# An attention and gated-MLP kernel rewritten: one batched Gelu per segment, 20 score fills, pooled PSUM banks, one bank for two projections, DMA transposes

## The chip, the cores and the metric

The kernel runs on one core of a Trainium2 chip. The metric is device time in microseconds (us) of that core. A ratio always uses runs of the kernel before taken on the same chip in the same rounds. "Ratio" is the mean time of one kernel's fast runs over the mean time of the other's fast runs of the same rounds, so it is not quite the ratio of the medians that are quoted beside it. "us more" or "us less" than the changed kernel is a difference of medians from different jobs on different chips.

The engines are named as in the profile: PE (TensorE matmuls), PEld (its weight loads), DVE (VectorE), ACT (ScalarE), POOL (GpSimd), SP (SyncE, which here only issues DMAs). The program lists the instructions of each engine in one order, which is fixed when the kernel is built, by a list scheduler with estimated durations.

## The reference, cut to what matters

Both branches read the same x, 2048 tokens of 512 features. Four segments of 512 tokens are handled in order.

```python
def _A_ref(x, wq, wk, wv, wo, beta):              # 32 heads of 16
    for s in range(4):                            # segments of 512 tokens
        logits = einsum('bhqd,bhkd->bhqk', qs, ks) * scale + mask   # causal
        a_dot  = einsum('bhqk,bhkd->bhqd', softmax(logits), vs)
        a_mem  = phi(qs) @ M / (phi(qs) @ z + 1e-6)                 # memory of earlier segments
        outs.append(g * a_mem + (1 - g) * a_dot)
        M, z = M + phi(ks).T @ vs, z + phi(ks).sum()
    return concat(outs) @ wo
def _B_ref(x, w_gate, w_up, w_down):              # hidden size 1792 = 14 blocks of 128
    return (gelu(x @ w_gate) * (x @ w_up)) @ w_down                 # tanh form of gelu
gate = sigmoid((x * gate_w).sum(-1))
out  = gate * _A_ref(x, ...) + (1 - gate) * _B_ref(x, ...)
```

## The kernel before

Three parts of it matter for what follows.

The first is Gelu. For each of 14 blocks in each of 4 segments, the gate and up projections land in one fixed PSUM bank each, and six steps alternate between ACT and DVE:

```python
gc1  ACT  gs = copy(Gb)                         # out of PSUM
gu   DVE  ws = gs * gs
gz   DVE  ws = (ws + 1/C3) * gs
gt   ACT  ws = tanh(C_TANH*C3 * ws)
gh   DVE  ws = (ws + 1) * gs
gf   DVE  hT[ft] = 0.5 * ws * Ub                # frees the up-projection's bank
```

The second is the softmax. Scores of four heads go to four PSUM banks `X[0..3]` (one tensor, `psXALL`), one exp reads all four, POOL zeroes what is above the diagonal. There are three fills per unit and eight units per segment, so 96 exps:

```python
FILLS = [("A", [(0, 512, 0)], 512),
         ("B", [(1, 384, 0), (3, 128, 384)], 512),
         ("C", [(2, 256, 0)], 256)]              # this exp is only half as wide
```

The third is the use of the eight PSUM banks: four for scores, one each for gate (`Gb`), up (`Ub`), value products (`Pb`) and everything else (`Mb`). The down-projection and the O-projection both use `Mb`, one after the other, with an eviction each. phi of the keys (the positive form that the memory uses) and the attention outputs are transposed by PE through PSUM.

```python
task(f"bev{s}_{tile}", DVE, bsb = Mb * omgt)          # down-projection out of PSUM
...                                                   # O-projection into Mb again
task(f"fin{s}_{tile}", DVE, ostage = Mb * omgt + bsb)
```

The softmax here doesn't subtract the row's maximum and nothing guards it: scores larger than these inputs give would overflow.

Of the kernel before, what the change touches and what calls it, by code (L numbers as in the profile page):

```python
# [8 lines left out]


class InstrSpec:
    __slots__ = ("fn", "reads", "writes", "est", "dma_sem", "dma_inc", "waits", "task", "deps", "inc", "ins_name", "lat")

    def __init__(self, fn, reads=(), writes=(), est=0.1, dma_sem=None, dma_inc=16, lat=0.0):
        self.fn = fn
        self.lat = lat
        self.reads = tuple(reads)
        self.writes = tuple(writes)
        self.est = est
        self.dma_sem = dma_sem  # L20
        self.dma_inc = dma_inc
        self.waits = []
        self.task = None
        self.deps = []
        self.inc = False
        self.ins_name = None


class Task:
    __slots__ = ("name", "eng", "instrs", "est", "reads", "writes", "preds", "succs",  # L30
                 "prio", "start", "finish", "id", "order_bias", "lock_bank", "lock_gid", "lock_last", "lat")

    def __init__(self, name, eng, instrs, order_bias=0.0, lock=None):
        self.name = name
        self.eng = eng
        self.lock_bank, self.lock_gid, self.lock_last = lock if lock is not None else (None, None, None)
        self.instrs = list(instrs)
        for i in self.instrs:
            i.task = self
        self.est = sum(i.est for i in self.instrs) + 1e-3  # L40
        self.lat = max([i.lat for i in self.instrs] + [0.0])
        rs, ws = set(), set()
        for i in self.instrs:
            rs.update(i.reads)
            ws.update(i.writes)
        self.reads = rs
        self.writes = ws
        self.preds = set()
        self.succs = set()
        self.prio = 0.0  # L50
        self.start = None
        self.finish = None
        self.id = None
        self.order_bias = order_bias


class Sched:
    def __init__(self):
        self.tasks = []
        self._res_w = {}  # L60
        self._res_r = defaultdict(set)

    def add(self, task):
        task.id = len(self.tasks)
        deps = set()
        for r in task.reads:
            w = self._res_w.get(r)
            if w is not None and w is not task:
                deps.add(w)
        for w in task.writes:  # L70
            lw = self._res_w.get(w)
            if lw is not None and lw is not task:
                deps.add(lw)
            for rt in self._res_r.get(w, ()):
                if rt is not task:
                    deps.add(rt)
        for d in deps:
            task.preds.add(d)
            d.succs.add(task)
        for r in task.reads:  # L80
            self._res_r[r].add(task)
        for w in task.writes:
            self._res_w[w] = task
            self._res_r[w] = set()
        self.tasks.append(task)
        return task

    def schedule(self):
        tasks = self.tasks
        for t in reversed(tasks):  # L90
            best = 0.0
            for s in t.succs:
                if s.prio > best:
                    best = s.prio
            t.prio = t.est + best + t.order_bias
        n = len(tasks)
        npred = [len(t.preds) for t in tasks]
        ready_time = [0.0] * n
        ready = {e: [] for e in ENGINES}
        for t in tasks:  # L100
            if npred[t.id] == 0:
                ready[t.eng].append(t.id)
        cur = {e: 0.0 for e in ENGINES}
        done = 0
        order = []
        locked = {}
        while done < n:
            best = None
            best_e = None
            for e in ENGINES:  # L110
                lst = ready[e]
                if not lst:
                    continue
                ce = cur[e]
                bt = None
                bkey = None
                for tid in lst:
                    tt = tasks[tid]
                    blocked = False
                    for bk, gid in locked.items():  # L120
                        if bk in tt.writes and gid != tt.lock_gid:
                            blocked = True
                            break
                    if blocked:
                        continue
                    rt = ready_time[tid]
                    k = ((rt if rt > ce else ce), -tasks[tid].prio, tid)
                    if bkey is None or k < bkey:
                        bkey = k
                        bt = tid  # L130
                key = bkey
                if best is None or key < best:
                    best = key
                    best_e = e
            assert best is not None, "deadlock in task graph"
            st, _, tid = best
            ready[best_e].remove(tid)
            t = tasks[tid]
            if t.lock_bank is not None:
                if t.lock_last:  # L140
                    locked.pop(t.lock_bank, None)
                else:
                    locked[t.lock_bank] = t.lock_gid
            t.start = st
            t.finish = st + t.est
            cur[best_e] = t.finish
            order.append(t)
            done += 1
            for sc in t.succs:
                npred[sc.id] -= 1  # L150
                rt = t.finish + t.lat
                if ready_time[sc.id] < rt:
                    ready_time[sc.id] = rt
                if npred[sc.id] == 0:
                    ready[sc.eng].append(sc.id)
        self.order = order
        self.makespan = max(cur.values())
        self.eng_busy = {e: sum(t.est for t in tasks if t.eng == e) for e in ENGINES}
# [3 lines left out]
class Emitter:  # L162

    def __init__(self, nc, engmap):
        self.nc = nc
        self.engmap = engmap
        self.cnt = {}
        for e in (PE, ACT, DVE, POOL):
            self.cnt[e] = nc.alloc_semaphore(f"cnt_{e}")
# [5 lines left out]
    def plan(self, eng, spec):  # L175
        res = self.res
        deps = []
        for r in spec.reads:
# [3 lines left out]
        for w in spec.writes:  # L182
            st = res.get(w)
            if st is None:
                continue
            if st[0] is not None:
                deps.append(st[0])
            deps.extend(st[1].values())
        spec.deps = deps
        if spec.dma_sem is not None:  # L190
            sem = spec.dma_sem
            cur = self.dma_val.get(sem, 0) + spec.dma_inc
            self.dma_val[sem] = cur
            ref = ("d", sem, cur)
            rkey = ("d", id(sem))
        else:
            idx = len(self.streams[eng])
            ref = ("c", eng, idx)
            rkey = ("c", eng)
        for r in spec.reads:  # L200
            st = res.get(r)
            if st is None:
                st = [None, {}]
                res[r] = st
            st[1][rkey] = ref
        for w in spec.writes:
            res[w] = [ref, {}]
        self.streams[eng].append(spec)
        self.order.append((eng, spec))
        return ref  # L210

    def finalize(self):
        needed = {e: set() for e in (PE, ACT, DVE, POOL)}
        for eng, spec in self.order:
            for d in spec.deps:
                if d[0] == "c":
                    _, pe_, idx = d
                    if pe_ == PE and eng == PE:
                        continue
                    needed[pe_].add(idx)  # L220
        val = {}
        for e in (PE, ACT, DVE, POOL):
            c = 0
            vals = []
            for i, spec in enumerate(self.streams[e]):
                if i in needed[e]:
                    c += 1
                    spec.inc = True
                else:
                    spec.inc = False  # L230
# [3 lines left out]
        for eng, spec in self.order:  # L234
            req = {}
            for d in spec.deps:
                if d[0] == "c":
                    _, pe_, idx = d
                    if pe_ == PE and eng == PE:
                        continue  # L240
                    sem = self.cnt[pe_]
                    v = val[pe_][idx]
                else:
                    _, sem, v = d
                k = id(sem)
                if k not in req or req[k][1] < v:
                    req[k] = (sem, v)
            w = waited[eng]
            waits = []
            for k, (sem, v) in req.items():  # L250
                if w.get(k, -1) < v:
                    waits.append((sem, v))
                    w[k] = v
            spec.waits = waits

    def emit_stream(self, eng):
        e = self.engmap[eng]
        for spec in self.streams[eng]:
            for sem, val in spec.waits:
                e.wait_ge(sem, val)  # L260
            ins = spec.fn(e)
            try:
                spec.ins_name = ins.ins.name
            except Exception:
                spec.ins_name = None
            if spec.dma_sem is not None:
                ins.then_inc(spec.dma_sem, spec.dma_inc)
            elif spec.inc:
# [691 lines left out]
```

## Time and profile before

| | before |
|---|---|
| median time | 383.34 us (382.6 to 384.04, 3 runs) |
| profiled span | 381.4 us |
| exps, mean | 64 of 1.873 us, 32 of 1.021 us |
| DVE in the Gelu steps | 42.9 + 40.8 + 38.1 + 28.9 = 150.7 us |
| table loads on ACT | 1 of 1.283 us |

From the profile's page of the kernel before, part 1: the busy time of each engine and its share of the span.

```profile
span 381.4 us, 7327 instructions
PE 308.6 (81%) x2955; PEld 143.0 (38%) x3002; DVE 294.3 (77%) x635; ACT 253.6 (66%) x286; POOL 97.5 (26%) x147
```

From the same page, part 4, the chain of work that ended last, followed back from the end and summed by engine.

```profile
DVE 44%; PE 26%; ACT 20%; issue 6%; SPq 1%; POOL 1%; DMA 1%; POOLq 0%; ACTq 0%; DVEq 0%
```

No engine is full, and the chain goes from engine to engine with DVE in front. The groups view of the kernel before, by form, shows what they are busy with. Its columns are line, engine, operation, output<-input, shapes, count, then busy us and mean ns of one, then the engine's idle time just before these instructions and what ended it.

```profile
L769 ACT ACTIVATE pt<-psXALL 128x2048 bf16<-128x2048 f32 x64 | 119.9, 1873 | 19.1 <-PE psXALL L759 17.0 <-PE psP L788 1.0 <-POOL pt L776 0.4
...
L734 DVE SCALAR_TENSOR_TENSOR ws<-ws,gs 128x512 bf16<-128x512 bf16 x56 | 42.9, 765 | 1.5
L740 DVE SCALAR_TENSOR_TENSOR ws<-ws,gs 128x512 bf16<-128x512 bf16 x56 | 40.8, 729 | 2.9 <-ACT ws L737 2.0
...
L743 DVE SCALAR_TENSOR_TENSOR hT<-ws,psU 128x512 bf16<-128x512 bf16 x56 | 38.1, 681 | 7.8 <-PE psU L725 7.5
L737 ACT ACTIVATE ws<-ws 128x512 bf16<-128x512 bf16 x56 | 34.5, 627 | 27.2 <-DVE ws L734 27.1
...
L731 DVE TENSOR_TENSOR ws<-gs 128x512 bf16<-128x512 bf16 x56 | 28.9, 516 | 9.3 <-ACT gs L729 9.1
```

L734 and L731 are the cubic and the square, L740 the product, L743 the last product. Half of DVE's 294 us is Gelu. The Tanh (L737) stands idle 27 us for the cubic. The waits view (who waited for whom, us in total, times, longest) shows how that travels on to PE:

```profile
ACT ws L737 <- DVE ws L734: 27.1, 25, 4.2
ACT pt L769 <- PE psXALL L759: 26.6, 36, 2.2
PEld psU L725 <- DVE hT L743: 17.2, 23, 1.6
```

PE cannot start the next up-projection before DVE has emptied `Ub`. The second line is another loop. The timeline of the kernel before, 6 us of it (start, duration, engine, line), shows one turn:

```profile
173.68 1.86 ACT L769 ACTIVATE pt<-psXALL 128x2048 bf16<-128x2048 f32 x1
...
175.59 0.40 PE L759 MATMUL psXALL<-qT,kpad_1 32*128 32x384 bf16 x8 [0.18 <-ACT pt L769]
...
176.18 1.88 ACT L769 ACTIVATE pt<-psXALL 128x2048 bf16<-128x2048 f32 x1 [0.64 <-PE psXALL L759]
```

An exp ends, the scores of the next fill are computed into the same four banks (0.40 us), the next exp starts. The turn takes 2.50 us, of which ACT works 1.88.

### The profile page before, as it was taken

The page shows a single profiled execution, that of the slowest core. Times are in us where ns is not written, and L with a number is a line of the kernel's source. Part 1 is how long each engine was busy: PE and PEld are TensorE (multiplying, and loading weights), DVE is VectorE, ACT ScalarE, POOL GpSimd, SP SyncE. Part 2 cuts the span into 40 slices and gives each one's busy share as a digit, 9 for nine tenths or more (in the row PEclk, how much of TensorE's full clock was granted, in tenths as well). Part 3 has the DMA queues.
Part 4 walks back from the last instruction along what each step waited for, and adds up shares of the span by engine and source line. Part 5 has one row for each costly group of instructions (what it writes and reads, how often), then busy time and mean ns, then how long its engine had stood idle before and what let it go on. Part 6 is the DMA issues. An engine that isn't in the chain of part 4 may idle for free.

```text
span 381.4 us, 7327 instructions
## 1 busy us (share of the span) xinstructions
PE 308.6 (81%) x2955; PEld 143.0 (38%) x3002; DVE 294.3 (77%) x635; ACT 253.6 (66%) x286; POOL 97.5 (26%) x147
## 2 busy tenths in 40 slices
PE   4798887989878679788998878687998987688854
PEld 1344343444333244333443334343443324334431
DVE  0479898877866999997589899998587599985333
ACT  1579899875567367787567947787837765867630
POOL 7003433440022023233200312333300220433320
PEclk9999999999999987999999999999999999989968
DMA  3997000020010000001001000000000100000001
GB/s 86 353 363 110 2 3 2 1 57 2 0 43 15 0 2 2 0 16 44 2 0 41 15 0 3 2 2 0 3 2 14 43 1 2 2 0 2 2 0 55
DMA packets 17744, 12.26 MB, mean 32 GB/s; under 512 B 9776, under 2 KB 17712, under 8 KB 17712
## 3 DMA queue, kind: packets, MB, share of 16 engines
q1 hardware_dynamic: 17712, 11.81, 10.8%
q8 instruction: 23, 0.38, 0.4%
q14 instruction: 9, 0.07, 0.1%
HBM read 7.61 MB, written 2.10 MB: 25 GB/s over the span
## 4 chain that ended last, share of the span: by engine, by line
DVE 44%; PE 26%; ACT 20%; issue 6%; SPq 1%; POOL 1%; DMA 1%; POOLq 0%; ACTq 0%; DVEq 0%
ACT pt L769 11%; DVE ws L734 6%; DVE ws L740 6%; DVE hT L743 5%; PE psU L725 4%; PE psXALL L759 4%; DVE ws L731 4%; PE psM L838 4%; PE psM L861 3%; ACT kpad_1 L575 3%; PE psG L719 3%; ACT kpad_0 L575 2%; DVE ost L866 2%; PE psP L788 2%; DVE scr L816 2%
## 5 line engine op out<-in xcount | busy, mean ns | idle before, releaser
L769 ACT ACTIVATE pt<-psXALL 128x2048 bf16<-128x2048 f32 (+1 forms) x96 | 152.5, 1589 | 30.6 <-PE psXALL L759 26.6
L776 POOL TENSOR_SCALAR_AFFINE_SELECT pt<-pt 128x512 bf16<-128x512 bf16 x128 | 90.6, 709 | 267.8 <-ACT pt L769 226.9
L725 PE MATMUL psU<-xT,wu 128*128 128x512 bf16 x207 | 55.7, 388 | 15.5 <-DVE hT L743 11.1
L719 PE MATMUL psG<-xT,wg 128*128 128x512 bf16 x210 | 56.1, 386 | 8.6 <-ACT gs L729 7.0
L838 PE MATMUL psM<-wd,hT 128*128 128x512 bf16 x213 | 52.8, 379 | 3.1 <-DVE bsb L843 1.9
L737 ACT ACTIVATE ws<-ws 128x512 bf16<-128x512 bf16 x56 | 34.5, 627 | 27.2 <-DVE ws L734 27.1
L788 PE MATMUL psP<-vaug,pt 128*128 128x17 bf16 x1280 | 46.1, 171 | 6.9 <-POOL pt L776 3.5
L788 PEld LDWEIGHTS psP<-vaug,pt 128*128 128x128 bf16 x1280 | 40.3, 96 | 30.2 <-issue 16.9
L729 ACT ACTIVATE gs<-psG 128x512 bf16<-128x512 f32 x56 | 33.2, 593 | 17.2 <-DVE ws L740 8.9
L743 DVE SCALAR_TENSOR_TENSOR hT<-ws,psU 128x512 bf16<-128x512 bf16 x56 | 38.1, 681 | 7.8 <-PE psU L725 7.5
L734 DVE SCALAR_TENSOR_TENSOR ws<-ws,gs 128x512 bf16<-128x512 bf16 x56 | 42.9, 765 | 1.5
L740 DVE SCALAR_TENSOR_TENSOR ws<-ws,gs 128x512 bf16<-128x512 bf16 x56 | 40.8, 729 | 2.9 <-ACT ws L737 2.0
L731 DVE TENSOR_TENSOR ws<-gs 128x512 bf16<-128x512 bf16 x56 | 28.9, 516 | 9.3 <-ACT gs L729 9.1
L725 PEld LDWEIGHTS psU<-xT,wu 128*128 128x128 bf16 x224 | 18.2, 99 | 34.9 <-DVE hT L743 17.2
L719 PEld LDWEIGHTS psG<-xT,wg 128*128 128x128 bf16 x224 | 18.6, 98 | 28.8 <-ACT gs L729 10.6
L838 PEld LDWEIGHTS psM<-wd,hT 128*128 128x128 bf16 x224 | 19.2, 97 | 22.7 <-DVE bsb L843 2.2
L759 PE MATMUL psXALL<-qT,kpad_0 32*128 32x512 bf16 (+3 forms) x256 | 17.4, 302 | 8.7 <-ACT pt L769 8.2
L861 PE MATMUL psM<-wo,oT 128*128 128x512 bf16 x62 | 16.8, 393 | 7.8 <-DVE ost L866 5.2
L759 PE MATMUL psXALL<-qT,kpad_1 32*128 32x512 bf16 (+3 forms) x256 | 17.8, 311 | 4.5 <-ACT pt L769 4.3
L566 PE MATMUL psXALL<-xT,wk 128*128 128x512 bf16 x64 | 15.5, 394 | 5.4 <-DMA wk<-in_A_wk_dram 5.4
L803 DVE RECIPROCAL recip<-psP 128x16 f32<-128x16 f32 x32 | 8.1, 254 | 14.5 <-PE psP L788 14.3
L570 DVE CAST kT<-psXALL 128x512 bf16<-128x512 f32 x16 | 11.0, 688 | 10.7 <-PE psXALL L566 10.3
(81 smaller groups left out, 311.4 us busy)
## 6 DMA issues: line engine op xcount, KB each, us to landing
out_dram<-ost SPq DMA_DIRECT2D x16, 128.0 KB, 1.7
wg<-in_B_w_gate_dram SPq DMA_DIRECT2D x2, 896.0 KB, 9.4
wu<-in_B_w_up_dram SPq DMA_DIRECT2D x2, 896.0 KB, 10.6
wd<-in_B_w_down_dram SPq DMA_DIRECT2D x1, 1792.0 KB, 16.4
wk<-in_A_wk_dram SPq DMA_DIRECT2D x1, 512.0 KB, 4.7
wv<-in_A_wv_dram SPq DMA_DIRECT2D x1, 512.0 KB, 5.6
wq<-in_A_wq_dram SPq DMA_DIRECT2D x1, 512.0 KB, 6.4
wo<-in_A_wo_dram SPq DMA_DIRECT2D x1, 512.0 KB, 16.4
```

Source lines behind the costliest of these rows:

```text
L719: instrs.append(I(lambda e, kb=kb, ft=ft: e.matmul(Gb[:, :], wg[:, kb, ft * 128:(ft + 1) * 128], xT[sl][:, kb, :], start=(kb == 0), stop=( ...
L725: instrs.append(I(lambda e, kb=kb, ft=ft: e.matmul(Ub[:, :], wu[:, kb, ft * 128:(ft + 1) * 128], xT[sl][:, kb, :], start=(kb == 0), stop=( ...
L731: task(f"gu_{s}_{ft}", DVE, [I(lambda e, q=q: e.tensor_tensor(wsb[q][:, :], gsb[q][:, :], gsb[q][:, :], ALU.mult), reads=[("gsb", q)], wri ...
L734: task(f"gz_{s}_{ft}", DVE, [I(lambda e, q=q: e.scalar_tensor_tensor(out=wsb[q][:, :], in0=wsb[q][:, :], scalar=1.0 / C3, in1=gsb[q][:, :] ...
L737: task(f"gt_{s}_{ft}", ACT, [I(lambda e, q=q: e.activation(wsb[q][:, :], wsb[q][:, :], ACTF.Tanh, scale=C_TANH * C3), reads=[("wsb", q)], ...
L740: task(f"gh_{s}_{ft}", DVE, [I(lambda e, q=q: e.scalar_tensor_tensor(out=wsb[q][:, :], in0=wsb[q][:, :], scalar=1.0, in1=gsb[q][:, :], op0 ...
L743: task(f"gf_{s}_{ft}", DVE, [I(lambda e, q=q, ft=ft: e.scalar_tensor_tensor(out=hT[:, ft, :], in0=wsb[q][:, :], scalar=0.5, in1=Ub[:, :], ...
L759: instrs.append(I(lambda e, g=g, t=t, kb=kb, ncol=ncol, c0=c0, kp=kp: e.matmul(X[g][:, c0:c0 + ncol], kp[32 * g:32 * g + 32, t, kb * 128:( ...
L769: task(f"exp{s}_{u}_{fname}", ACT, [I(lambda e, slot=slot, ncols=ncols, xin=xin: e.activation(PT[slot][:, :, 0:ncols], xin, ACTF.Exp, scal ...
L776: minstrs.append(I(lambda e, mview=mview: e.affine_select(out=mview, in_=mview, compare_op=ALU.is_ge, fill=0.0, base=0, pattern=[[0, 4], [ ...
L788: instrs.append(I(lambda e, qb=qb, kb=kb, g=g, h=h, slot=slot, c0=c0: e.matmul(Pb[:, (qb * 4 + g) * 17:(qb * 4 + g) * 17 + 17], PT[slot][: ...
L838: instrs.append(I(lambda e, fb=fb, tile=tile: e.matmul(Mb[:, :], hT[:, fb, tile * 128:(tile + 1) * 128], wd[:, fb, :], start=(fb == 0), st ...
```

## The change

The intent is to take the Gelu arithmetic off DVE, to make fewer exps and all of them wide, to let all PE groups share the remaining banks, and to move transposes from PE to the DMA engines. The whole builder and its scheduler were rewritten, so the diff is 1500 lines. Its core, cut and condensed:

```diff
@@ Gelu: gate blocks are copied to hT, then one function in four chunks per segment @@
-  gc1, gu, gz, gt, gh, gf                       # six steps per block, see above
+  copy_out(f"Gev{s}_{ft}", ..., hT[sl][:, ft, :])             # by ACT or DVE, as the scheduler likes
+  CHUNKS = [(0, 2), (2, 6), (6, 10), (10, 14)]
+  e.activation(hT[sl][:, f0:f1, :], hT[sl][:, f0:f1, :], ACTF.Gelu_apprx_tanh)
+       # after = all exps of the segment; exps of the next segment come after the last chunk
+  task(f"Um{s}_{ft}", DVE, hT[ft] = up_bank * hT[ft])
@@ scores: 5 full fills per pair of units (20 per segment) in place of 6 @@
-  3 fills per unit, the third 256 columns wide
+  a0 = fill("A0", [(0, 0, 512, 0)], [0])
+  b0 = fill("B0", [(0, 1, 384, 0), (0, 3, 128, 384)], [0, 384])
+  cc = fill("C", [(0, 2, 256, 0), (1, 2, 256, 256)], [(0, 256)])   # both units
+  a1, b1 likewise
@@ PSUM: N_W = 3 pooled work banks; a group gets a bank when the scheduler starts it @@
-  Pb, Gb, Ub, Mb
+  Pb, banks = [psW0, psW1, psW2]
@@ O-projection and down-projection accumulate in one bank, one eviction @@
-  bev: bsb = Mb * omgt ; fin: ostage = Mb * omgt + bsb
+  ins  = [wo matmuls, start at kb == 0] + [wd matmuls, stop at fb == NFT - 1]
+  fin: ostage = bank * omgt                                    # ACT or DVE
@@ transposes of phi(k) and of the attention output (not the last segment's) @@
-  PE transpose into PSUM, DVE copy
+  e.dma_start_transpose(phkt[:, :, t*128:(t+1)*128], phk[:, t, :])
+  e.dma_start_transpose(oT[:, :, qt*128:(qt+1)*128], otok[sl][:, qt, :])
@@ start: weights of keys, queries, values on ACT's DMA queue, x on SP's @@
+  wdma("wk", ACT, ...); xdma(0); wdma("wq", ACT, ...); ...; wdma("wv", ACT, ...)
@@ phi is computed on two blocks at a time, padded keys are made from SBUF by DVE,
   denominators of the memory term in one small group, evictions may run on ACT or DVE,
   the scheduler adds hand-over times, a DMA model and bank allocation @@
```

## The prediction

> **What bounds it now.** No engine is full. The page gives a 381.4 us span: PE busy 308.6 (81%), DVE 294.3 (77%), ACT 253.6 (66%). The chain that ended last is 44% DVE, 26% PE, 20% ACT. The groups view shows why: each of the 56 Gelu blocks costs six steps that alternate between ACT and DVE: square 0.52, cubic 0.77, product 0.73, final product 0.68 us (2.7 us DVE), copy 0.59 and Tanh 0.63 us (1.2 us ACT). DVE Gelu work is 150.7 us. The waits view: Tanh waits 27 us for DVE, the up-projection's bank 17+11 us for the final DVE product. The timeline shows a second loop: the four score banks are single, so exp to exp is 1.88 + about 0.64 us (exp end, four score matmuls 0.4 us, exp).
>
> **Removed.** Square, cubic, product: 112.6 us DVE. Tanh: 34.5 us ACT. 16 down-projection evictions: 12.0 us DVE. Key padding from PSUM: 22 us ACT, replaced by a few us of DVE on wide SBUF operands. 24 phi and 12 output PE transposes with 12+12 DVE copies (about 10 us).
>
> **Added or moved.** One Gelu per 14 blocks, in four chunks: by the 0.83 us per 1000 elements that the 2048-wide exp's and 512-wide Tanh's times imply, about 6.8 us a segment, 27 us. Exp and this Gelu are, by the Trainium skill ("ScalarE: Activation LUTs", Table sets), likely in different table sets: 8 loads instead of 1. The trace's load took 1.283 us, as that page says; about 9 us more. Exp: 64x1873+32x1021 ns becomes 80x1873: 150 against 152.6 us: merging saves starts, not exp work.
>
> Estimated totals: ACT fixed work 200, DVE fixed work 125, movable evictions about 79 us: some 205 each. PE streaming hardly falls: 928 matmuls of 512 at 0.216 us (four in 0.87 us) is 200; value products 1280x0.027 = 35; scores about 20; rest 10: about 265 us. PE becomes the most loaded engine, the exp loop close behind.
>
> **Critical path, by stage.** Start: key weights are issued on ACT beside the transposes, so the first exp comes at about 13.5 us. Each segment has 20 exps at 2.52 us, plus about 0.25 us for scores queued behind other matmuls: 55 us; plus wide phi exps (6, 4, 2 of 1.05 us) and Gelu with two loads, 9.4 us. Segments: 70, 68, 66 us; PE needs about 66 in the middle ones, so it is nearly tied. Last exps 55. Then an exposed tail: Gelu, up-projection 12.3, down-projection 15.6, output 3: 34 us. Sum: 307 us. DVE's 150 us of relief thus gives about 75, because the exp loop and PE take over.
>
> **Prediction: 307 us, range 288 to 328.** Faster by over 2%: 0.96; within: 0.03; slower: 0.01.
>
> **Checks.** DVE busy 170 to 215 us, ACT 195 to 225, PE busy share 88% or more; 8 table loads; Gelu group near 27 us; exp x80 near 1.87 us with about 0.6 us idle before each; chain led by PE and ACT, DVE below 20%; no exp in the last 30 to 36 us.
>
> **What would make it wrong.** A fixed instruction order that fits reality badly: score matmuls held behind work matmuls whose bank is not free (three work banks), making exp gaps over 1 us. Transposing DMAs on one queue holding output or the memory products. Evictions assigned to ACT blocking exps. Gelu sharing exp's table, or PE filling the gaps better, would give 285 to 295.

## The result, and the profile after

The median is 317.69 us (315.19 to 318.75, 4 runs) against 383.09 us. The ratio is 0.8248, with a 95% interval from 0.8187 to 0.8309. Executions over 1.5% slower than the fastest of the same kernel are left out of the means. The prediction's range of 288 to 328 us holds it; the time is 10.7 us above the point of 307.

The kernel after, page parts 1 and 4, as shown of before:

```profile
span 315.7 us, 6866 instructions
PE 291.3 (92%) x2952; PEld 137.3 (43%) x2952; DVE 178.5 (57%) x360; ACT 219.7 (70%) x163; POOL 87.4 (28%) x130
...
PE 74%; DVE 10%; ACT 9%; DMA 3%; issue 2%; POOL 1%; SPq 0%; ACTq 0%; DVEq 0%
```

DVE lost 116 us and went from 44% to 10% of the chain. PE lost 17 us of busy time and now makes up three quarters of the chain. The groups view of the kernel after, by form:

```profile
L635 ACT ACTIVATE pt<-psXALL 128x2048 bf16<-128x2048 f32 x80 | 150.1, 1876 | 43.8 <-PE psXALL L628 39.3 <-POOL pt L646 4.2
...
L748 DVE TENSOR_TENSOR hT<-psW,hT 128x512 bf16<-128x512 f32 x56 | 37.0, 688 | 20.1 <-PE psW L372 20.0
L389 DVE CAST hT<-psW 128x512 bf16<-128x512 f32 x43 | 29.1, 689 | 11.8 <-PE psW L372 11.6
L733 ACT ACTIVATE hT<-hT 128x2048 bf16<-128x2048 bf16 x12 | 22.0, 1893 | 0.0
...
L733 ACT ACT_TABLE_LOAD x4 | 5.1, 1283 | 0.1
...
L635 ACT ACT_TABLE_LOAD x3 | 3.8, 1283 | 0.1
```

The Gelu chunks and the exps force seven more table loads of 1.283 us each. The last product (L748) now waits for PE; before, PE waited for it. The waits view after, for the two waits that answer to those of before (the Tanh's has no successor):

```profile
ACT pt L635 <- PE psXALL L628: 39.3, 44, 2.0
...
PEld psW L372 <- DVE hT L748: 3.6, 10, 0.8
```

The most useful view of this kernel is the table of windows, cut at the events that the program has in each segment: the first exp (17.13 us), and the Gelu stretch of each segment, from its table load to the next one's end. The columns are the stretch, its length, then busy us and instruction count of each engine, the granted TensorE clock, DMA share and GB/s.

```profile
0.00:17.13 17.13, 9.65 (x31) 3.12 (x32) 2.88 (x9) 3.97 (x7) 6.37 (x18) 0.80 0.96 202
17.13:76.88 59.75, 57.73 (x683) 28.36 (x682) 43.30 (x92) 51.08 (x46) 20.29 (x27) 1.00 0.46 115
76.88:85.92 9.04, 8.69 (x75) 3.89 (x72) 6.49 (x12) 9.01 (x6) 1.07 (x2) 1.00 0.29 58
85.92:141.54 55.62, 50.09 (x585) 23.77 (x583) 39.78 (x82) 41.43 (x26) 18.66 (x26) 0.94 0.12 23
141.54:150.60 9.06, 7.94 (x70) 3.82 (x71) 2.07 (x6) 9.02 (x6) 1.27 (x2) 1.00 0.21 49
150.60:207.06 56.46, 54.28 (x631) 26.35 (x629) 41.02 (x82) 42.62 (x29) 18.83 (x26) 0.97 0.04 10
207.06:216.11 9.05, 8.04 (x72) 3.98 (x72) 3.36 (x8) 9.02 (x6) 1.27 (x2) 1.00 0.08 16
216.11:272.71 56.60, 54.99 (x590) 25.24 (x588) 26.16 (x53) 40.65 (x28) 18.35 (x26) 1.00 0.07 18
272.71:315.70 42.99, 39.85 (x229) 18.72 (x227) 13.46 (x22) 12.88 (x13) 1.27 (x2) 0.99 0.08 25
```

Four stretches of 20 exps take 55.6 to 59.8 us each, with PE 90 to 97% busy in them. After the last exp there are 43.0 us more (the tail), in which ACT is busy for 12.9 us, 7.7 of them the last Gelu and its table load, and PE for 39.9 us, 93%. Of this tail PE spends 100 matmuls on the down-projection. One segment has 56, so 44 of them belong to the segment before. They are a backlog: work that the program did not place among the exps and that PE does at the end.

### The profile page after: what moved, and what is told of

Its sections match the earlier page's. It is cut to its first block, busy times and chain, and to the rows that moved or that the text cites. A ratio compares the mean times of both kernels' runs of the same rounds, so it can differ in the third digit from the quotient of the medians.

```text
span 315.7 us, 6866 instructions
## 1 busy us (share of the span) xinstructions
PE 291.3 (92%) x2952; PEld 137.3 (43%) x2952; DVE 178.5 (57%) x360; ACT 219.7 (70%) x163; POOL 87.4 (28%) x130
## 4 chain that ended last, share of the span: by engine, by line
PE 74%; DVE 10%; ACT 9%; DMA 3%; issue 2%; POOL 1%; SPq 0%; ACTq 0%; DVEq 0%
PE psW L372 59%; PE psP L670 8%; PE psXALL L628 7%; ACT pt L635 6%; DMA xT<-in_A_x_dram 3%; ACT hT L733 2%; DVE pex L509 1%; POOL pt L646 1%; DVE hT L389 1%; DVE ost L766 1%; DVE phk L511 1%; DVE vaug L389 1%; DVE ndsc L570 1%; DVE hT L748 1%; DVE qT L389 0%
## 5 line engine op out<-in xcount | busy, mean ns | idle before, releaser
L635 ACT ACTIVATE pt<-psXALL 128x2048 bf16<-128x2048 f32 x80 | 150.1, 1876 | 43.8 <-PE psXALL L628 39.3
L646 POOL TENSOR_SCALAR_AFFINE_SELECT pt<-pt 128x512 bf16<-128x512 bf16 (+1 forms) x112 | 81.0, 723 | 185.5 <-ACT pt L635 175.9
L372 PE MATMUL psW<-xT,wg 128*128 128x512 bf16 x224 | 57.0, 380 | 1.1 <-DVE hT L389 1.0
L372 PE MATMUL psW<-xT,wu 128*128 128x512 bf16 x224 | 57.4, 392 | 0.0
L372 PE MATMUL psW<-wd,hT 128*128 128x512 bf16 x224 | 54.8, 379 | 0.0
L748 DVE TENSOR_TENSOR hT<-psW,hT 128x512 bf16<-128x512 f32 x56 | 37.0, 688 | 20.1 <-PE psW L372 20.0
L389 DVE CAST hT<-psW 128x512 bf16<-128x512 f32 x43 | 29.1, 689 | 11.8 <-PE psW L372 11.6
L372 PEld LDWEIGHTS psW<-wd,hT 128*128 128x128 bf16 x224 | 20.8, 97 | 23.2 <-issue 0.6
L684 DVE RECIPROCAL recip<-psP 128x16 f32<-128x16 f32 x32 | 8.2, 255 | 39.3 <-PE psP L670 39.3
L372 PEld LDWEIGHTS psW<-xT,wu 128*128 128x128 bf16 x224 | 19.0, 99 | 23.9 <-issue 5.1
L733 ACT ACTIVATE hT<-hT 128x2048 bf16<-128x2048 bf16 (+1 forms) x16 | 25.8, 1684 | 0.0
L763 ACT ACTIVATE ost<-psW,omgt 128x512 bf16<-128x512 f32 x7 | 4.8, 687 | 17.4 <-PE psW L372 15.8
```

Source lines behind the costliest of these rows:

```text
L372: return Instr(lambda e: e.matmul(view(), lhsT, rhs, start=first, stop=last), reads=reads, writes=[fkey if fkey is not None else g.key], e ...
L389: alts[DVE] = [Instr(lambda e: e.tensor_copy(dst(), src()), reads=reads, writes=writes, est=dve_t(n))]
L635: prev_exp[0] = exp_task(s, f"exp{s}_{t}{name}", [Instr(lambda e: e.activation(PT[slot][:], XALL[:, :].rearrange("p (g c) -> p g c", g=4), ...
L646: minstrs.append(Instr(lambda e, view=view, pat=pat: e.affine_select(out=view, in_=view, compare_op=ALU.is_ge, fill=0.0, base=0, pattern=p ...
L684: Instr(lambda e: e.reciprocal(recip[i2][:], Pb[:, 16:272:17]), [("P",)], [("recip", i2)], 0.25),
L733: lambda e, f0=f0, f1=f1: e.activation(hT[sl][:, f0:f1, :], hT[sl][:, f0:f1, :], ACTF.Gelu_apprx_tanh), hk, hk,
```

## The experiments

Twelve kernels were run, each with three timed rounds beside the kernel before. The main question was what bounds the kernel now; then which part of the rewrite brought how much; then whether what was found gives a faster kernel. Two things should be kept in mind. The program's order is computed anew for every kernel, so an undone part also changes the order of everything else. And an output inside the tolerance is weak evidence for the MLP branch: the runs e1_halfup and e6_onestep compute it wrongly and still passed, while e3_noswitch, wrong there too, failed with a relative error of 0.022.

Theory P says that PE is the limit after the start. Theory E, its rival, says that the loop of scores and exp is.

### e1_halfup: less work for PE

```diff
-  ... wu[:, kb, ...], xT ..., kb == 0, kb == 3, 512) for kb in range(4)]
+  ... wu[:, kb, ...], xT ..., kb == 0, kb == 1, 512) for kb in range(2)]
```

> Wrong result on purpose: the up-projection contracts only two of its four blocks, so the tensor engine loses 112 matmuls of 512 columns (112 x 0.216 = 24 us) and nothing else changes. Theory P (tensor engine is the limit after the start): 290 to 298 us, 20 to 26 us less. Theory E (the loop score matmuls, exp, score matmuls is the limit, the tensor engine only fills its gaps): only the exposed part after the last exp gets shorter, about 6 us for 28 matmuls, so 308 to 313 us.

Measured: 304.66 us (ratio 0.7927, 0.7896 to 0.7958), 13.0 us less than the changed kernel's 317.69. Neither theory had it. The windows of this run, after the last exp:

```profile
268.87:301.80 32.93, 28.97 (x167) 12.19 (x168) 12.38 (x22) 11.47 (x11) 1.27 (x2) 1.00 0.07 25
```

The tail went from 43.0 to 32.9 us, and the last Gelu starts only 3.8 us earlier, at 268.9. So the stretches with exps hardly moved with 18 us less of matmuls in front of that point, while the tail gave back what was taken from it (28 matmuls, 6 us) and more than half of its backlog: it holds 73 down-projection matmuls, 17 of the segment before, where the changed kernel has 44.

### e2_halfexp: less work for ACT

```diff
-  PT[slot][:],           X.rearrange(...)            # exp, 4 x 512 columns
+  PT[slot][:, :, 0:256], X.rearrange(...)[:, :, 0:256]
```

> Wrong result on purpose: each exp works on 256 of 512 columns of each bank, so ScalarE loses 80 x 0.85 = 68 us and the tensor engine does the same work (start-up memsets on VectorE fill the unwritten halves before the first exp). Theory P: 307 to 318 us, at most the 10 us of tensor engine gaps that waits for exp leave. Theory E: each loop gets 0.85 us shorter, 250 to 275 us.

Measured: 307.25 us (ratio 0.8012, 0.7973 to 0.8050), 10.4 us less, as theory P had it. The last two windows of this run, split at the last Gelu's table load:

```profile
163.44:231.64 68.20, 65.10 (x726) 32.97 (x737) 37.03 (x78) 38.02 (x40) 19.98 (x28) 1.00 0.08 15
231.64:305.50 73.86, 70.41 (x368) 32.46 (x373) 26.73 (x42) 18.16 (x21) 0.00 (x0) 1.00 0.06 19
```

The last Gelu starts 41 us earlier and the tail is 31 us longer, with PE busy 95% of it. (The first exp comes 2.9 us later than in the changed kernel, at 20.0 us, in a program with more DVE work at the start, so the stretches gave up 44 us.) The exp loop had set the pace of the stretches, but some three quarters of what it gives up goes into the PE backlog. Together the two runs say that neither theory alone is right: **time = start + four stretches paced by the exp loop + a tail that holds the PE work left behind the last exp**. Taking 24 us of PE work or 68 us of exp work brings 13 and 10 us.

### e3_noswitch: without the table loads

```diff
-  ACTF.Gelu_apprx_tanh
+  ACTF.Tanh
```

> Wrong result on purpose: Tanh in place of Gelu in the same four chunks per segment, so the 7 table loads between Gelu and exp (9.0 us of ScalarE) go away and the order rules stay. Theory P: 314 to 318 us, under 1% less, as the tensor engine is 86 to 96% busy during the loads. Theory E: 306 to 310 us, 8 to 9 us less.

Measured: 311.5 us (ratio 0.8107, 0.8077 to 0.8137), 6.2 us less. The seven loads cost 9.0 us of ACT. Six of them, 7.7 us, lie before the last Gelu starts; it started 5.9 us earlier, and the tail stayed as it was, 43.1 us. The time lies between the two theories, which fits the sum above: the loads lengthen the stretches. Here nothing of what the stretches gave up went into the tail.

### e4_startorder: who shares the DMA engines at the start

```diff
-  wdma("wq", ACT, ...); wdma("beta", ACT, ...); wdma("gatew", ACT, ...); wdma("wv", ACT, ...)
+  wdma("wq", SP,  ...); wdma("beta", SP,  ...); wdma("gatew", SP,  ...); wdma("wv", SP,  ...)   # behind x(0)
```

> Only the key weights are loaded from ScalarE's queue; wq, beta, the gate vector and wv are issued on SyncE's queue behind the four transposing loads of the first x block, so that these share the DMA engines with 0.5 MB instead of 1.5 MB. Theory P and a start that is held by the transposing loads: steady matmuls begin at about 9 us instead of 12.6, and the whole time falls by about as much, to 313 to 315 us. Rival (the transposing loads are slow by themselves, not by company): no change, 317 us, or slower if wq is then late.

The changed kernel's chain in time order shows the start, the third number being what ran:

```profile
2.09 9.20 DMA xT<-in_A_x_dram
11.34 5.34 PE psW L372 x17
```

One transposing load of 128 KB took 9.2 us to land beside 1.5 MB of weights. Measured: 314.4 us (ratio 0.8189, 0.8155 to 0.8224). The timeline of ACT in this run:

```profile
13.94 1.88 ACT L635 ACTIVATE pt<-psXALL 128x2048 bf16<-128x2048 f32 x1 [0.20 <-PE psXALL L628]
```

The first exp comes at 13.94 instead of 17.13 us, 3.2 us earlier, and the median is 3.3 us lower. The intervals of the two kernels' ratios overlap, so the gain in whole time is likely rather than shown; the earlier first exp is in the trace. The last piece of x that a key matmul waited for was there at 6.3 us, where the slow load above landed at 11.3. The expected steady matmuls from 9 us came, but in part at half pace: the key matmuls, which waited only 2.1 us for x, ran from 6.7 to 10.5 us at one each 0.43 us, twice the 0.216 us of later. The query matmuls followed at 11.6 us without a wait for wq, and the value matmuls waited 0.7 to 0.9 us for wv. So the earlier start gained less than it might have, because the matmuls were still slow. Why they were is not shown: the granted clock that this trace gives for the stretch is 1.00. The Trainium skill ("DMA: Bandwidth & Descriptors", Rules for kernel authors) says that spreading DMAs over issuing engines does not help bandwidth, since they run on the same 16 DMA engines and interleave. This fits that: with 1.5 MB of weights issued from ACT beside them, the pieces of x that PE needed first landed up to 5 us later than with 0.5 MB.

### e5_tanhchain: the old Gelu in the new frame

```diff
-  copy_out(Gev -> hT); gelu chunks; Um: hT = bank * hT
+  copy_out(-> gs); gu, gz (DVE); gt: Tanh (ACT); gh (DVE) -> hT; Um: hT = 0.5 * hT * bank
```

> The changed kernel with the six-step Tanh form of Gelu of the kernel before put back, per block of 128 hidden units; all else (banks, fills, DMA transposes, order search) as changed. Same result. Adds 56 x (0.52+0.77+0.73) = 113 us of VectorE and 35 - 27 - 9 = 0 us of ScalarE. Theory D (the gain is the relief of VectorE): VectorE gets to some 290 us, time 350 to 375 us. Rival S (the gain is the pooled banks and the order search): 320 to 335 us.

Measured: 361.89 us (ratio 0.9423, 0.9402 to 0.9443), 44.2 us more than the changed kernel. Theory D, that the relief of DVE matters most, is right about the direction and size. Page part 1 of this run:

```profile
PE 307.6 (85%) x2952; PEld 143.3 (40%) x2952; DVE 260.5 (72%) x506; ACT 226.8 (63%) x218; POOL 94.9 (26%) x130
```

DVE rose to 260.5 us and not 290. In part this is because the scheduler gave ACT 28 of the 56 gate evictions instead of 13 (18.7 us of them on DVE instead of 29.1); the rest is not traced. And not all of the 44.2 us need be DVE's: the same 2952 matmuls kept PE busy for 307.6 us instead of 291.3, at a mean granted clock of 0.924 instead of 0.972. What the lower clock costs is not separated from what the waits for DVE cost.

### e6_onestep: a cheap Gelu in the old frame

```diff
-  gc1 (copy), gu, gz, gt (Tanh), gh
+  ws = tanh(Gb)                       # ACT, straight out of PSUM; wrong on purpose
   gf: hT = 0.5 * ws * Ub
```

> Wrong result on purpose: the kernel before, with copy, square, cubic, Tanh and product of Gelu replaced by one Tanh out of PSUM (113 us of VectorE and 34 us of ScalarE less, no table loads), all else in its old form; its order is computed anew. Theory D: 315 to 330 us, nearly all of the gain. Rival S: 350 us or more, as the single G and U banks and 96 exps remain.

Measured: 353.64 us (ratio 0.9210, 0.9188 to 0.9231), 30.3 us less than before. DVE busy fell to 192.7 us, about what it is after the change, and yet less than half of the 65 us came. Rival S had this one: without the new fills and banks the relief of DVE is worth 30 us, though this run also takes 28 us off ACT and needs no table loads between exp and Gelu, which the real change does need. The chain of this run (page, part 4) tells what took over:

```profile
PE 42%; ACT 31%; DVE 15%; issue 6%; POOL 2%; SPq 2%; DMA 1%; ACTq 0%; POOLq 0%; DVEq 0%
```

The chain's largest line is the exp with 21%. That the 96 exps with their hand-overs pace the old frame is a reading of this chain; no run tests it.

### e7_twobanks: two work banks

```diff
-N_W = 3
+N_W = 2
```

> Two pooled work banks in place of three, nothing else. If the pool matters: a group of four matmuls (0.87 us) and its eviction (0.6 to 0.7 us plus about 0.25 us of hand-over) must alternate on two banks, and down-projection groups hold one for long, so 330 to 345 us. If it does not: 316 to 322 us.

Measured: a median of 339.53 us, but two of the four runs (340.07 and 340.4 us) were slow. The fast two took 334.54 and 339.0 us, and by their ratio (0.8771, 0.8702 to 0.8841) the kernel is about 20 us slower than the changed one. The window after the last exp, from the run of 334.54 us:

```profile
267.81:332.80 64.99, 60.49 (x312) 25.18 (x309) 24.28 (x38) 12.88 (x13) 1.27 (x2) 1.00 0.05 17
```

The exps even ended earlier than with three banks, 267.8 against 272.7. With two banks PE gets less done between the exps, and the tail grows from 43 to 65 us: it now holds all 112 up-projection and all 112 down-projection matmuls of the last two segments. So the pool's worth does not show in the loop: it is in the backlog.

### e8_24fills: the third fill split again

```diff
-  cc = fill("C", [(0, 2, 256, 0), (1, 2, 256, 256)], [(0, 256)])
+  c0 = fill("C0", [(0, 2, 256, 0)], [0], 256)      # and c1 for the other unit
```

> The third score fill is split per head group again: 64 exps of 2048 and 32 of 1024 columns, as before the change (ScalarE +2.6 us, 16 more hand-overs of 0.5 to 0.6 us in the exp loop, a few more tensor engine switches). If the exp loop sets the pace of the four segments: 324 to 328 us, 7 to 11 us more. If the tensor engine alone does: 317 to 320 us.

Measured: 328.17 us (ratio 0.8560, 0.8527 to 0.8592), 10.5 us more, as expected if the loop paces the stretches. The last Gelu's table load starts at 286.2 instead of 272.7 us; the tail is 42.5 us, unchanged. ACT's exp work grew by only 120.1 + 32.7 - 150.1 = 2.7 us. The rest, 7.8 us, fits 16 more hand-overs in the loop at 0.5 us each.

One thing about the tail can be seen here. These are its windows in e3_noswitch and in this run:

```profile
266.84:309.90 43.06, 39.74 (x225) 18.83 (x227) 13.46 (x22) 11.57 (x13) 1.27 (x2) 0.99 0.08 25
286.23:328.70 42.47, 39.36 (x226) 18.51 (x224) 12.94 (x21) 13.56 (x14) 0.64 (x1) 1.00 0.08 26
```

From the first exp to the last, e3_noswitch takes 5.6 us less than the changed kernel and this run 13.0 us more, and yet both have the changed kernel's tail of 43.0 us, with nearly the same matmuls in it (99 and 97 of the down-projection, against 100). Slower stretches did not let PE catch up. How much is left behind the last exp is settled when the order is computed, with estimated durations. From the first exp to the last Gelu's start PE is idle for 13.8 us in the changed kernel, so an order with a smaller backlog may be possible; no run tries one.

### e9_sepO: two banks and two evictions per output tile

```diff
-  ins = wo matmuls + wd matmuls in one bank; fin: ostage = bank * omgt
+  wd matmuls in bank 1; bev: bsb = bank1 * omgt (DVE)
+  wo matmuls in bank 2; fin: ostage = bank2 * omgt + bsb (DVE)
```

> O-projection and down-projection go back to two banks with two evictions (scale on the way out, then scale and add), as before the change; nothing else. Adds 16 VectorE evictions (12 us) and 16 bank hand-overs, no matmul. Both theories (tensor engine and exp loop as joint limits, VectorE with much slack): 317 to 321 us, under 1% more, most of it in the tail. If bank pressure matters here too: 324 us or more.

Measured: 325.91 us (ratio 0.8486, 0.8437 to 0.8536), 8.2 us more. The expectation of 317 to 321 us was wrong; its other branch, bank pressure, is the one that fits. No matmul was added. In this run's trace the exps end 3.3 us later and the tail is 48.7 instead of 43.0 us, with 190 up-, down- and O-projection matmuls in it instead of 177 (13 x 0.216 = 2.8 us of backlog). The rest of the difference is not traced to single waits. Since the order was computed anew, part of it may be the order and not the banks; that stays open.

### e10_petr: transposes back on PE

```diff
-  e.dma_start_transpose(phkt..., phk...), e.dma_start_transpose(oT..., otok...)
+  PE transpose into a pooled bank, copied out by ACT or DVE
```

> The 24 DMA transposes between on-chip buffers go back to the tensor engine (96 transposes of 128 columns, about 5.5 us of tensor engine by the 0.055 us a transpose that their streaming takes, plus 24 copies out through the pooled banks). If the tensor engine's total counts almost in full: 321 to 325 us. If it disappears in gaps: 316 to 319 us.

Measured: 324.63 us (ratio 0.8456, 0.8422 to 0.8490), 6.9 us more. The 5.5 us of PE count in full, and a little more with the hand-overs. It ends at the upper edge of the expected 321 to 325.

### e11_plainx: the first x block transposed by the idle PE

```diff
-  xdma(0)                              # four transposing loads
+  dma(xr[:, t, :] <- x rows of tile t) # four plain loads, then 16 PE transposes, 4 copies to xT[0]
+  # and the other weights behind it on SP, as in e4_startorder
```

> Candidate for a faster version: the first x block is loaded plainly and transposed by the idle tensor engine (16 transposes, 4 copies), with the other weights behind it on SyncE's queue as in the start-order run. If the start adds in full to the end time, as the start-order run showed (first exp 3.2 us earlier, whole 3.3 us less): first exp at 10.5 to 11.5 us instead of 17.1, whole 311 to 313 us. If something else then holds the start (weights): 313 to 316 us.

Measured: 313.54 us (ratio 0.8179, 0.8133 to 0.8225). The first exp comes at 13.44 us. The expectation of 10.5 to 11.5 us failed: the plain 128 KB loads took 4.4 us (median), the transposes ran from 4.8 us (all but the first from 5.9 us) to about 8 us, and the first key matmul ran at 8.0 us after the copies. Half a microsecond over e4_startorder is what was left. The whole time is at the border between its two branches.

### e12_pool4: the value-product bank joins the pool

```diff
-N_W = 3;  Pb = psum_tensor("psP")
+N_W = 4;  each unit's value products take a bank from the pool, one unit at a time
```

> Candidate on top of the plain first load: the bank of the value products joins the pool, four work banks shared by all (one unit's value products at a time), so that other work has four banks when no value products are open. Two banks in place of three cost 22 us. If a fourth still helps: 306 to 311 us against 313.5. If three were enough: 312 to 316 us.

Measured: 309.51 us (309.28 to 311.57, ratio 0.8073, 0.8038 to 0.8109), on top of e11_plainx. The intervals of the two do not meet. A fourth bank still helps, by 4.0 us, again in the tail (39.2 instead of 43.0 us). This version is correct and beats both kernels.

### One table of all of them

The last Gelu's table load marks the end of the exps (for e3_noswitch, which has none, the start of the last Gelu stretch). All from the profiled execution of each kernel, in us.

| kernel | first exp | exps over at | tail | span | median |
|---|---|---|---|---|---|
| after | 17.1 | 272.7 | 43.0 | 315.7 | 317.69 |
| e1_halfup (PE -24) | 15.8 | 268.9 | 32.9 | 301.8 | 304.66 |
| e2_halfexp (ACT -68) | 20.0 | 231.6 | 73.9 | 305.5 | 307.25 |
| e3_noswitch (ACT -9) | 16.9 | 266.8 | 43.1 | 309.9 | 311.5 |
| e4_startorder | 13.9 | 267.9 | 42.9 | 310.8 | 314.4 |
| e7_twobanks | 17.6 | 267.8 | 65.0 | 332.8 | 339.53 (two of four slow) |
| e8_24fills | 17.7 | 286.2 | 42.5 | 328.7 | 328.17 |
| e9_sepO | 17.7 | 276.0 | 48.7 | 324.7 | 325.91 |
| e10_petr (PE +5.5) | 17.5 | 276.8 | 46.3 | 323.1 | 324.63 |
| e11_plainx | 13.4 | 267.7 | 43.0 | 310.7 | 313.54 |
| e12_pool4 | 13.5 | 268.4 | 39.2 | 307.6 | 309.51 |

The single parts undone cost 44.2 (batched Gelu), about 20 (third work bank), 10.5 (merged fills), 8.2 (one bank for two projections) and 6.9 us (DMA transposes). They add up to some 90 us, more than the 65.4 us of the whole. The parts need each other, so these are not shares of the gain.

## Why the prediction was right or wrong

- **The direction and size held.** "DVE's 150 us of relief thus gives about 75, because the exp loop and PE take over": the gain was 65.4 us of medians, and e1_halfup, e2_halfexp and the windows show both successors at work. But the sentence gives the whole gain to DVE's relief, and the runs do not: a cheap Gelu in the old frame brought 30 us (e6_onestep), and the third bank, the merged fills, the shared bank and the DMA transposes cost 7 to 20 us each when undone. DVE's busy time fell by 116 us and not 150, since the 38 us of the last product stayed (37.0 us after) and evictions moved to DVE.
- **The checks were met, but one.** DVE 178.5 us (170 to 215), ACT 219.7 (195 to 225), PE 92% (88 or more), 8 table loads, Gelu 25.8 us (near 27), exps of 1.876 us with 43.8/80 = 0.55 us idle before each, a chain of PE with DVE at 10%. "No exp in the last 30 to 36 us" was missed: it is 43.0.
- **The start was mis-sized.** "The first exp comes at about 13.5 us": 17.1. The step that failed is "key weights are issued on ACT beside the transposes, so": the company of 1.5 MB made a transposing load take 9.2 us, and e4_startorder, which takes the company away, has its first exp at 13.9.
- **The stretches were well sized.** Predicted 70, 68, 66 and 55 us, measured from the windows 68.8, 64.7, 65.5 and 56.6 (each with its Gelu, the last without).
- **The tail was mis-sized.** "Then an exposed tail: ... 34 us": 43.0. The term that was too small is the down-projection, 15.6 us for one segment's 72 matmuls (56 and 16 of the O-projection). The tail held 44 more down-projection matmuls and some of the O-projection of the segment before, some 10 us of backlog. The prediction had treated each segment as the larger of PE and ACT time and let PE catch up. PE's streaming was put at 265 us, and with the exps made half as long, e2_halfexp still shows 284 us of busy PE in a span of 305.5: PE is busier than the estimate said. Part of the matmuls ran at half clock (in the changed kernel 5 us on end, see the last section); the rest of the difference is not worked out.
- Start +3.6, stretches -3.4, tail +9.0 give 9.2 us over the 306.5 that the terms sum to, and that is the span of 315.7. That the first two cancel is luck: nothing ties the late start to the short stretches.
- **A count was off without effect on the sum.** The prediction has "24 phi and 12 output PE transposes"; the trace of before has 48 and 64, of which the change takes 48 and 48 away. What they cost in time (e10_petr: 6.9 us) is within the "about 10 us" that the prediction gave for PE and copies.
- **A rate does not follow from its source.** The "0.83 us per 1000 elements" of the Gelu estimate comes out of the two exps, (1873 - 1021) ns for 1024 columns; exp against Tanh, the pair that the prediction names, gives (1873 - 627) ns for 1536, or 0.81. Either gives about 27 us; measured 25.8.
- **What would make it wrong** named score matmuls held behind work matmuls whose bank is not free. The waits view has ACT waiting 39.3 us for scores, and e7_twobanks shows that banks matter, though through the backlog and not through the loop.

## What to carry to other kernels

When a loop with a single buffer paces one engine and another engine fills its gaps, add up three terms instead of taking a maximum: the start, the paced stretches, and the filler's work that the order leaves for the end. A change that speeds up the loop may then move work into that tail (e2_halfexp, three quarters of the gain) or leave it alone (e3_noswitch), since a fixed order decides what waits at the end; and a change that costs the filler may show in the tail (e7_twobanks), or in both (e10_petr: 3.3 us in the tail, 3.8 in the stretches). So look at the end of the trace before judging what a change did. Undo parts one at a time before crediting the largest: here, taking the Gelu steps off DVE was worth 30 us in the old frame and 44 in the new one, and parts that looked like tidying (a bank, a merged fill, an eviction) were worth 7 to 20 us each.

## What the Trainium skill lacked or had wrong

- "TensorE: Matmul & The Clock Gate", Back-to-back issue gap, gives 131 ns per matmul of 512 columns as a sustained figure for a stream with weight loads. No run here shows that: in the tail of the kernel after, 26 such matmuls in a row took 5.78 us, the last 0.38 of it its own length, so (5.78 - 0.38) / 25 = 0.216 us each, which is the page's figure for an isolated gap.
- The same page, Part 1, says that the clock halves after an idle window of about 3.4 us. Here it was halved after no such gap; the page's passage on a second failure mode, short idles between groups of matmuls, is nearer to this. In the windows view of the kernel after, PE was 71% busy from 104.0 to 107.5 us, and then had half the clock for 5 us on end. The mean clock of 0.86 in the first line shows that the change falls inside it; finer windows put it at 106.6 us. In the 3.4 us up to 106.5 PE was busy for 1.98 us, 58%, with small matmuls of few columns, and its longest idle wait was 0.79 us:

```profile
104.00:107.50 3.50, 2.48 (x48) 1.45 (x47) 3.43 (x8) 1.95 (x2) 2.07 (x3) 0.86 0.69 79
107.50:112.50 5.00, 4.96 (x50) 2.37 (x51) 3.61 (x8) 3.22 (x2) 0.98 (x2) 0.50 0.01 2
```

- "ScalarE: Activation LUTs", Table sets, lists gelu in a set other than exp's and says that the tanh form of gelu is separate from gelu's, but does not name the set of the tanh form. The trace shows that exp and this Gelu do not share one: 8 loads, 1.283 us each, as the page says. The page adds 1.38 us of drain to each switch. These traces do not show it: in the timeline the exp before ends at 207.05, the load starts at 207.06 and the first Gelu chunk at 208.35, 1.29 us after it, and e3_noswitch gains 6.2 us for seven loads, less than 1 us a load.
- "DMA: Bandwidth & Descriptors" has no figure for what plain loads do to a transposing load beside them. Here one of 128 KB took 9.2 us to land beside 1.5 MB of weights; with 0.5 MB beside them the first exp came 3.2 us earlier.
- No page has a rule for the tail that a paced loop leaves behind on another engine, which was worth 9 us of the prediction's error.
